# Row maxima of an attention kernel computed in one step per period, partly in spare columns of the scores' PSUM banks

## The chip, the cores and the metric

The kernel runs on one core of a Trainium2 chip. The metric is the device time of one execution in microseconds. The engines are called by the names of the profile: PE is TensorE's matmuls and PEld its weight loads, DVE is VectorE, ACT is ScalarE, POOL is GpSimd, SP is SyncE, which here only issues DMAs.

## What is computed

Two blocks follow each other. The first is attention with routing over 4 batches, 8 heads, 768 positions and head dimension 64. Each query and each key is assigned to the nearest of 16 centroids of its head, and a query sees only the keys of its own cluster. The second is a feed-forward layer on 3,072 tokens with the gate h * erf(softplus(h)).

```
mask   = q_assign[:, :, :, None] == k_assign[:, :, None, :]
scores = scale * q @ k.T
scores = where(mask, scores, -1e9)
attn   = exp(scores - max(scores)); attn /= sum(attn) + 1e-9
x      = (attn @ v) reshaped to (3072, 512)
h      = x @ w_in            # 512 -> 2048
out    = (h * erf(softplus(h))) @ w_out
```

This document is about the `max(scores)` of the first block: for every query a value to subtract ahead of the exponential.

## The kernel before, in words

**Pairs, units and periods.** Two heads are worked on together as a pair; there are 16 pairs (`NPAIR`). The two heads lie on partitions 0 to 63 and 64 to 127 of every operand, so that their matmuls use different rows of the array and run beside each other (`e` is 0 or 1 in the code). A pair's queries are cut into two halves of 384 (`HW`), its keys into six tiles of 128 (`NJ`). A unit `u` is one tile of keys against one half of the queries, so a pair has 12 units. A period (`period(p, i)`, line 1023) does two units, and a pair has six periods, i = 0 to 5. The order of instructions is the one in which the code is written: all engines are wrapped in `InOrder` (line 116), which keeps program order on each of them. Waits between engines are not written by hand: the tile framework puts them in, from the tiles that instructions read and write.

**A unit's way.** `products(u)` (line 500) multiplies a tile of keys with half the queries in fp32 and puts the result into a buffer `sc` of two PSUM banks, one for each head, 384 of 512 columns in each. `scores(u)` (line 513) adds a bf16 matmul of `km` and `qm` into the same columns: one row of them carries the shift (the maximum to be subtracted), the others the routing mask as very large numbers. `curve(u)` (line 527) is the exponential on ScalarE, from `sc` into a buffer `pr`. `attend(u)` (line 548) multiplies it with the values, one period later, into a bank `turned`; `accumulate(u)` (line 536) sums the exponentials on GpSimd, and `divide` (line 561) finishes a half: a matmul with `minus`, two curves on ScalarE, then three steps on VectorE.

**The maxima, three periods ahead.** `maxima_step(p, i)` (line 449) forms the bf16 scores again in the other orientation, 128 queries (a query tile t) on the partitions against 384 keys in the columns, in two passes, `qv` with `kv` (the scores themselves) and `qm` with `km` (the mask). Its output is `wide`, a tile of two PSUM banks, of which 384 columns each are used. VectorE reduces it to the maxima `nmx`. `step_ahead(u)` (line 1010) calls it for a step that lies 6 units ahead. Each period has two such steps: one for the first half of the keys, at its start, and one for the second half, whose passes are put around `scores` (`second`, lines 1050 to 1063). The second pass of the latter uses only rows 32 to 63 of each head's 64, so that it runs beside `scores`, which uses rows 0 to 31. When three query tiles are done, `lowest` takes the smallest over the pieces (the values are negated), and `turn` (line 480, called at i = 0 and 3) brings them into a row: six matmuls with an identity into `turned`, and two copies on ScalarE of one row each into row 0 of `qm`. The `scores` of the same period read that row.

**What lies around it in a period.** In the order of the code: `turn` and the first step ahead; a mask matmul (`mask(0)`); part of `divide`; the products of both units; `mask(1)`; the second step's first pass; scores; the rest of the second step; `mask(2)`; the two exponentials; preparation of weights for the second block on ScalarE, VectorE and GpSimd (`bounded`, `sign`, `shifted`, `size_and_rest`, `summed`, in most pairs); routing of a later pair (`choose`, `similarities`, `vectors`, `transposes`); then `accumulate`, `attend` and `divide` of the two units before. `choose` (line 393) writes its group maxima into columns 488 to 511 of a score buffer, which nothing else uses.

**PSUM.** Eight banks: two are `turned`, two are `wide` (line 175), and four are the two buffers of pool `ps_s` (line 174), which hands them out as tiles `sc` in turn (line 505).

Of the kernel before, what the change touches and what calls it, by code (L numbers as in the profile page):

```python
# [9 lines left out]
F32 = mybir.dt.float32  # L10
# [4 lines left out]
ALU = mybir.AluOpType  # L15
ACT = mybir.ActivationFunctionType
AX = mybir.AxisListType
PSUM = bass.MemoryType.PSUM

P = 128  # L20
B, H, S, D = 4, 8, 768, 64
C = 16
NJ = S // P
Q = 32
NB = S // Q
HW = S // 2
QW = HW // 2
TW = QW + 2
HJ = NJ // 2
HP = H // 2  # L30
NPAIR = B * HP
# [101 lines left out]
def kernel(  # L133
# [13 lines left out]
    te, ve, ae, ge = (  # L147
        InOrder(tc, e, in_order) for e in (nc.tensor, nc.vector, nc.scalar, nc.gpsimd)
    )
# [8 lines left out]
    turned = [ps.tile([P, 512], F32, name=f"turned{i}") for i in range(2)]  # L158
# [12 lines left out]
    def passing(name, bufs, **kw):  # L171
        return attention.enter_context(tc.tile_pool(name=name, bufs=bufs, **kw))

    ps_s = passing("ps_s", 2, space=PSUM)
    wide = passing("ps_w", 1, space=PSUM).tile([P, 2, 512], F32, name="wide")

    const = passing("fixed", 1)
# [12 lines left out]
    lowest = [const.tile([P, HJ, P], BF16, name=f"lowest{i}") for i in range(2)]  # L190
# [255 lines left out]

    turns = []

    def maxima_step(p, i, sm=wide, behind=False):

        st = pairs[p]
        nmx = maxima[p % 2]
        t, half = divmod(i, 2)

        def passes(a, b, start, rows):
            for e in range(2):
                r = slice(e * D + rows.start, e * D + rows.stop)
                te.matmul(
                    sm[:, e, 0:HW], lhsT=st[a][r, t * P : (t + 1) * P],
                    rhs=st[b][r, half * HW : (half + 1) * HW], start=start, stop=not start,  # L460
                )

        passes("qv", "kv", True, slice(0, D))
        if behind:
            yield
        passes("qm", "km", False, slice(Q, D) if behind else slice(0, D))
        if behind:
            yield
        ve.tensor_reduce(
            out=nmx[:, :, t, half], in_=sm[:, :, 0:HW], axis=AX.X, op=ALU.max, negate=True  # L470
        )
        if i in (NJ - 1, 2 * NJ - 1):
            h = i // NJ
            ve.tensor_reduce(
                out=lowest[h][:, :, ::D].rearrange("p t e -> p e t"),
                in_=nmx[:, :, h * HJ : (h + 1) * HJ], axis=AX.X, op=ALU.min,
            )
            turns.append((p, h))

    def turn(p, h, copies=(ae.copy, ae.copy)):  # L480

        st = pairs[p]
        pn = turned[h][:, 0:HW].rearrange("p (t n) -> p t n", t=HJ)
        for t in range(HJ):
            for e in range(2):
                cols = slice(e * D, e * D + Q)
                te.matmul(pn[cols, t], lhsT=lowest[h][:, t, cols], rhs=identb, start=True, stop=True)
        for e, copy in zip(range(2), copies):
            r = slice(e * D, e * D + 1)
            copy(out=st["qm"][r, h * HW : (h + 1) * HW], in_=pn[r].rearrange("p t n -> p (t n)"))  # L490
        st["shift", h] = True
# [8 lines left out]
    def products(u):  # L500
        p, half, j = units[u]
        if u in sc_of:
            return
        st = pairs[p]
        sc = sc_of[u] = ps_s.tile([P, 2, 512], F32, name="sc", tag="s")
        for e in range(2):
            r = slice(e * D, (e + 1) * D)
            te.matmul(
                sc[:, e, 0:HW], lhsT=st["kT"][r, j * P : (j + 1) * P],
                rhs=st["qT"][r, half * HW : (half + 1) * HW], start=True, stop=False,  # L510
            )

    def scores(u, rows=Q):

        p, half, j = units[u]
        st = pairs[p]
        sc = sc_of[u]
        assert ("shift", half) in st
        for e in range(2):
            r = slice(e * D, (e + 1) * D)  # L520
            r = slice(r.start, r.start + rows)
            te.matmul(
                sc[:, e, 0:HW], lhsT=st["km"][r, j * P : (j + 1) * P],
                rhs=st["qm"][r, half * HW : (half + 1) * HW], start=False, stop=True,
            )
# [478 lines left out]
    def run(work):  # L1004
        for _ in work:
            pass

    def step_ahead(u, behind=False):  # L1010
        p, i = divmod(u + NJ, 2 * NJ)
        steps = maxima_step(p, i, behind=behind) if p < NPAIR else iter(())
        if not behind:
            run(steps)
        return steps

    forms = []
    for f in range(0, HF, 2):
        forms += zip(*(left_forms(e, *w_in_parts(f, 2)) for e in (ve, ge)))
# [3 lines left out]
    def period(p, i):  # L1023
        u = 2 * NJ * p + 2 * i
        n1, n2 = 2 * p - 1, 2 * p
        early = lambda n: 0 <= n < N_EARLY

        def mask(place):
            which = (MASKS if p else FIRST_MASKS).get((i, place))
            if which:  # L1030
                return masks(p + 1, *which, turned[0 if i in (0, 5) else 1], place > 1, ve if i == 0 else ae)
            return lambda: None

        if u > 0:
            for which in turns if i in (0, 3) else ():
                turn(*which)
                turns.remove(which)
            step_ahead(u)
        mask(0)()
        next(part[0], None)  # L1040
        if i == 5:
            next(routing[0], None)
        if i == 0 and p:
            run(routing[0])
        if u == 2:
            next(routing[0])
        products(u)
        products(u + 1)
        mask(1)()
        second = step_ahead(u + 1, True) if u > 0 else iter(())  # L1050
        next(second, None)
        rows = D if u == 0 or u + NJ >= len(units) else Q
        scores(u, rows)
        next(second, None)
        if i:
            next(second, None)
        next(part[0], None)
        scores(u + 1, rows)
        later = mask(2)
        if i == 0:  # L1060
            later()
            later = lambda: None
            next(second, None)
        if i == 3:
            similarities(p + 2)
            routing[0] = choose(p + 2, sc_of[u + 1][:, 0], True)
        curve(u)
        later()
        curve(u + 1)
        if u == 0:  # L1070
            step_ahead(1)
            similarities(1)
            routing[0] = choose(1, turned[0])
            next(routing[0])
            next(routing[0])
            vectors(1, "q")
            vectors(1, "k")
        if i == 0 and early(n1 - 1):
            bounded(n1 - 1)
            shifted(n1 - 1)  # L1080
            sign(n1 - 1)
        elif i == 1 and early(n1):
            size_and_rest(n1)
        elif i == 3 and early(n1):
            bounded(n1)
            sign(n1)
        elif i == 5 and early(n2):
            rest(n2)
        for _ in range(min(len(forms), FORMS.get(p, {}).get(i, 0))):
            forms.pop(0)[0]()  # L1090
        if i == 3:
            next(routing[0], None)
            if early(n1):
                shifted(n1)
            for _ in range(2):
                next(routing[0], None)
        elif i == 1:
            load(p + 1, "v", v, vp)
            if p == 0:
                run(routing[0])  # L1100
                transposes(2, "q")
        elif i == 2:
            transposes(p + 2, "k")
        elif i == 4:
            vectors(p + 2, "k")
            vectors(p + 2, "q")
        elif i == 5:
            transposes(p + 3, "q")
        if u > 0:
            if i == 1 and early(n1 - 1):  # L1110
                summed(n1 - 1)
            elif i == 4 and early(n1):
                summed(n1)
            for w in (u - 2, u - 1):
                accumulate(w)
            if i % HJ == 1 and p in POOL_FORMS and forms:
                forms.pop(0)[1]()
            for w in (u - 2, u - 1):
                attend(w)
            if i % HJ == 0:  # L1120
                part[0] = divide(u - 1)
                next(part[0])
        if i == 3 and early(n2):
            size(n2)
# [25 lines left out]
    for r in (0, D):  # L1150
        for half in range(2):
            for e in range(2):
# [2 lines left out]
                    out=pick[r : r + D, half, e * D : (e + 1) * D].rearrange("p (n c) -> p n c", n=2)[:, :, 1 : C + 1],  # L1155
                    in_=first[r : r + D, c : c + C].unsqueeze(1).to_broadcast([D, 2, C]),
                )
    also = ps_s.tile([P, 2, 512], F32, name="sc", tag="s")
    products(0)
    warm(9, turned[0], zeros)  # L1160
    run(choose(0))
# [9 lines left out]
    for n in range(PLACES - 1):  # L1171
        fetch(n)
    for i in range(NJ):
        run(maxima_step(0, i, also if i % 2 else wide))
        if i == 1:
            masks(0, "q", 1, turned[1])()
        if i < NJ - 1:
            warm(2, turned[0], zeros)
    step_ahead(0)
    warm(2, turned[0], zeros)  # L1180
    turn(0, 0, (ae.copy, ve.tensor_copy))
    turns.clear()
# [124 lines left out]
```

## Time and profile before

| | |
|---|---|
| median of 3 runs | 978.78 us (978.75 to 978.95) |
| the profiled execution | 978.7 us |
| its span on the core | 976.8 us |
| attention stage | up to about 408.5 us of the span |
| feed-forward stage | from about 408.5 us on |
| one pair of heads, for example 90.54 to 115.00 us | 24.46 us |
| TensorE busy in the span | 968.1 us |
| VectorE busy in the span | 757.9 us |
| ScalarE busy in the span | 526.8 us |
| one reduction of `wide` (768 elements per partition) | 955 ns on average |
| one exponential (768 elements per partition) | 812 ns on average |

How to read it: almost every instruction has the line of the helper that records it (124), so groups are told apart by the names of tiles, written as output <- inputs. In a group's line stand its count, then its busy time and the mean length of one, then the idle time of its engine just ahead of it and what ended that idle time. A timeline line has its start, its length, its engine, what it does, how many instructions are merged in it, and in brackets the idle time before them. In the table of waits stand the total, the number of times and the longest. Where a stretch of the span is given, its columns are the length of the stretch, then each engine's busy time (PE, PEld, DVE, ACT, POOL), the granted clock of TensorE, the share of the DMA engines and GB/s.

### The profile page before, as it was taken

The numbers are of one execution on the slowest core, as the hardware profiler recorded it, in microseconds if no ns is written. First come the engines' busy times: TensorE is split into PE (matmuls) and PEld (weight loads), VectorE is DVE, ScalarE is ACT, GpSimd is POOL, SyncE is SP. The second block draws the span as 40 slices with busy tenths as digits, with TensorE's granted clock in tenths as the row PEclk, the third lists the DMA queues.
The fourth block names the chain that finished last, engine by engine and source line by source line (L and its number), as shares of the span: only waits on it lengthen the run. The fifth ranks groups of instructions, "written<-read, shape, count | busy, mean of one in ns | idle before, by whom it ended". The sixth has DMA issues, their size and how long they took to land.

```text
span 976.8 us, 20838 instructions
## 1 busy us (share of the span) xinstructions
PE 968.1 (99%) x8282; PEld 724.4 (74%) x8282; DVE 757.9 (78%) x1431; ACT 526.8 (54%) x799; POOL 409.9 (42%) x277
## 2 busy tenths in 40 slices
PE   8999999999999999999999999999999999999998
PEld 3555555555555555688888888888888888888887
DVE  8888888888888886879788786568666856685766
ACT  3777777777777665377623430562165235413541
POOL 1688887788888888853199600000000000000000
PEclk9999999999999999999999999999999999999999
DMA  9444444444444211142004544023302420241023
GB/s 216 81 110 110 109 109 109 107 110 109 87 110 110 54 35 34 47 152 87 0 22 173 200 140 134 1 65 129 108 0 87 129 87 1 65 145 50 1 86 108
DMA packets 157185, 88.42 MB, mean 91 GB/s; under 512 B 129696, under 2 KB 139424, under 8 KB 157088
## 3 DMA queue, kind: packets, MB, share of 16 engines
q1 hardware_dynamic: 154736, 86.80, 32.2%
q8 instruction: 65, 1.06, 0.5%
q10 hardware_dynamic: 2352, 0.30, 0.2%
q14 instruction: 32, 0.26, 0.1%
HBM read 68.19 MB, written 18.87 MB: 89 GB/s over the span
## 4 chain that ended last, share of the span: by engine, by line
PE 97%; DVE 1%; SPq 1%; issue 0%; DMA 0%; ACT 0%; DVEq 0%
PE bank L124 43%; PE turned L124 31%; PE sc L124 17%; PE wide L124 6%; SPq L124 1%; DVE nmx L124 1%; DMA in_q<-in_q_dram 0%; DVE kT L124 0%; DVE qT L124 0%; DVE km L124 0%; DVE turned L124 0%; DVE sims L124 0%; ACT qm L124 0%; DVE g_more L124 0%; DVE osb L124 0%
## 5 line engine op out<-in xcount | busy, mean ns | idle before, releaser
L124 POOL TENSOR_TENSOR more_out<-more_out,pr 128x768 f32<-128x768 f32 x128 | 217.0, 1696 | 18.7 <-ACT pr L124 10.1
L124 DVE TENSOR_REDUCE nmx<-wide 128x2 f32<-128x768 f32 x189 | 180.5, 955 | 48.2 <-PE wide L124 47.2
L124 ACT ACTIVATE pr<-sc 128x768 f32<-128x768 f32 x192 | 148.9, 812 | 94.2 <-PE wide L124 78.6
L124 PE MATMUL turned<-pr,in_v 128*32 128x194 f32 x3072 | 145.5, 330 | 0.0
L124 DVE TENSOR_TENSOR g<-bank,g 128x256 f32<-128x256 f32 x222 | 89.5, 419 | 54.5 <-PE bank L124 34.6
L124 PEld LDWEIGHTS turned<-pr,in_v 128*32 128x32 f32 x3072 | 91.5, 109 | 51.2 <-issue 21.3
L124 DVE TENSOR_TENSOR g<-g 128x512 f32<-128x512 f32 x114 | 78.8, 692 | 42.3 <-PE bank L124 32.2
L124 PE MATMUL bank<-x_own,w_in 128*128 128x256 f32 x424 | 104.4, 379 | 0.0
L124 PE MATMUL sc<-qT,kT 64*128 64x384 f32 x528 | 98.3, 486 | 0.0
L124 PEld LDWEIGHTS bank<-x_own,w_in 128*128 128x128 f32 x424 | 80.4, 190 | 11.5 <-issue 0.6
L124 ACT ACT_TABLE_LOAD x48 | 61.6, 1283 | 38.2 <-DVE g L124 37.5
L124 DVE TENSOR_TENSOR g<-a_s,g 128x512 f32<-128x512 f32 x96 | 74.1, 786 | 3.8 <-ACT a_s L124 3.8
L124 PE MATMUL bank<-x_more,more_in 128*128 128x256 f32 x296 | 76.0, 379 | 0.0
L124 PE MATMUL bank<-w_out,g 128*128 128x256 f32 x328 | 75.7, 379 | 0.0
L124 POOL TENSOR_TENSOR more_out<-pr,pr 128x768 f32<-128x768 f32 x32 | 60.2, 1880 | 28.3 <-ACT pr L124 28.3
L124 PE MATMUL bank<-g_more,g 128*128 128x256 f32 x296 | 69.9, 379 | 0.0
L124 PEld LDWEIGHTS bank<-w_out,g 128*128 128x128 f32 x328 | 62.3, 190 | 8.5
L124 PEld LDWEIGHTS <-qv 64*128 64x128 bf16 x384 | 27.0, 93 | 52.8 <-issue 36.7
L124 PEld LDWEIGHTS sc<-qT,kT 64*128 64x128 f32 x528 | 50.0, 187 | 21.2 <-ACT inv L124 2.3
L124 PE MATMUL wide<-kv,qv 64*128 64x384 bf16 x378 | 64.1, 328 | 1.3 <-DVE nmx L124 0.6
L124 PE MATMUL wide<-km,qm 64*128 64x384 bf16 (+1 forms) x378 | 62.6, 327 | 0.0
L124 PEld LDWEIGHTS bank<-g_more,g 128*128 128x128 f32 x296 | 56.2, 190 | 7.6
(195 smaller groups left out, 1746.1 us busy)
## 6 DMA issues: line engine op xcount, KB each, us to landing
g_more<-b_dram SPq DMA_DIRECT2D x48, 512.0 KB, 3.3
x_own<-in_moe_w_in_dram SPq DMA_DIRECT2D x13, 512.0 KB, 4.5
in_v<-in_v_dram SPq DMA_DIRECT2D x32, 192.0 KB, 3.1
x_dram<-more_out SPq DMA_DIRECT2D x128, 48.0 KB, 2.0
x_own<-x_dram SPq DMA_DIRECT2D x6, 1024.0 KB, 5.3
in_k<-in_k_dram SPq DMA_DIRECT2D x59, 96.0 KB, 2.8
in_q<-in_q_dram SPq DMA_DIRECT2D x58, 96.0 KB, 2.8
out_dram<-osb SPq DMA_DIRECT2D x20, 256.0 KB, 3.3
```

Of the source, the lines that this page charges most:

```text
L124: ins = getattr(self.engine, name)(*args, **kw)
```

## The change

Five things change, all within the attention stage.

- The four banks of the scores become one tile `sc4`, taken once: two units by two heads by 512 columns. The buffer of unit u is `sc4[:, u % 2]`. The 128 columns from 384 on (`HW:`) in each of the four banks were spare.
- A period now finds the maxima of one query tile over all 768 keys in one step, `bounds(p, t)`: keys 0 to 511 in the two banks of `wide`, keys 512 to 639 in the spare columns of the even unit's banks, and 640 to 767 in those of the odd unit's banks. Two reductions follow, one of 1,024 elements per partition over `wide`, one of 512 over all four spare pieces. Before there were two of 768.
- The passes of the step are put in one bf16 group behind the products: first pass for `wide` and both spare pieces, then the second passes and the scores. All second passes use 32 rows: `wide` rows 32 to 63, the spare pieces rows 0 to 31, as the scores do. [...]
- `turn` and `mask(0)` move from before the products to behind them. Products are now the first matmuls of a period.
- `choose` for pair p + 2 puts its group maxima into the same columns of `turned[0]` rather than of a score buffer.

The last pair's later periods, which have no maxima to find, and the start of the kernel keep the old steps. The core of the diff:

```diff
-    ps_s = passing("ps_s", 2, space=PSUM)
+    sc4 = passing("ps_s", 1, space=PSUM).tile([P, 2, 2, 512], F32, name="sc")
...
+    def bounds(p, t):
+
+        st, nmx = pairs[p], maxima[p % 2]
+        outs = {"wide": wide, 0: sc4[:, 0, :, HW:], 1: sc4[:, 1, :, HW:]}
+        keys = {"wide": slice(0, 512), 0: slice(512, 512 + P), 1: slice(512 + P, S)}
+
+        def passes(at, a, b, rows, start, stop):
+            for e in range(2):
+                r = slice(e * D + rows.start, e * D + rows.stop)
+                te.matmul(
+                    outs[at][:, e], lhsT=st[a][r, t * P : (t + 1) * P], rhs=st[b][r, keys[at]],
+                    start=start, stop=stop,
+                )
+
+        def first_of(at):
+            passes(at, "qv", "kv", slice(0, D), at == "wide", False)
+
+        def second_of(at):
+            beside = at == "wide"
+            passes(at, "qm", "km", slice(Q, D) if beside else slice(0, Q), False, beside)
+
+        def reduced():
+            ve.tensor_reduce(out=nmx[:, :, t, 0], in_=wide, axis=AX.X, op=ALU.max, negate=True)
+            ve.tensor_reduce(
+                out=nmx[:, :, t, 1:3].rearrange("p e c -> p c e"), in_=sc4[:, :, :, HW:],
+                axis=AX.X, op=ALU.max, negate=True,
+            )
+            if t % HJ == HJ - 1:
+                lowest_of(p, t // HJ)
+
+        return first_of, second_of, reduced
...
-        sc = sc_of[u] = ps_s.tile([P, 2, 512], F32, name="sc", tag="s")
+        sc = sc_of[u] = sc4[:, u % 2]
...
-        if u > 0:
-            for which in turns if i in (0, 3) else ():
-                turn(*which)
-                turns.remove(which)
-            step_ahead(u)
-        mask(0)()
         next(part[0], None)
...
         products(u)
         products(u + 1)
-        mask(1)()
-        second = step_ahead(u + 1, True) if u > 0 else iter(())
-        next(second, None)
-        rows = D if u == 0 or u + NJ >= len(units) else Q
-        scores(u, rows)
-        next(second, None)
-        if i:
-            next(second, None)
-        next(part[0], None)
-        scores(u + 1, rows)
+        for which in turns if i in (0, 3) else ():
+            turn(*which)
+            turns.remove(which)
+        mask(0)()
+        ahead, tile_of = divmod(i + HJ, NJ)
+        ahead += p
+        if u == 0 or ahead >= NPAIR:
+            mask(1)()
+            scores(u, D)
+            scores(u + 1, D)
+            reduced = lambda: None
+        else:
+            first_of, second_of, reduced = bounds(ahead, tile_of)
+            for at in ("wide", 0, 1):
+                first_of(at)
+            mask(1)()
+            if i in (0, 3):
+                for at in (0, "wide", 1):
+                    second_of(at)
+                scores(u)
+                scores(u + 1)
+            else:
+                second_of("wide")
+                second_of(0)
+                scores(u)
+                second_of(1)
+                scores(u + 1)
         later = mask(2)
         if i == 0:
             later()
             later = lambda: None
-            next(second, None)
+        reduced()
+        next(part[0], None)
         if i == 3:
             similarities(p + 2)
-            routing[0] = choose(p + 2, sc_of[u + 1][:, 0], True)
+            routing[0] = choose(p + 2, turned[0], True)
         curve(u)
         later()
         curve(u + 1)
```

## The prediction

> **What bounds the kernel now.** I read the page first, then the waits and the busy times of the attention stage, then the timeline of single periods. The page's busy times and its chain of work, with two of its groups:
>
> ```profile
> PE 968.1 (99%) x8282; PEld 724.4 (74%) x8282; DVE 757.9 (78%) x1431; ACT 526.8 (54%) x799; POOL 409.9 (42%) x277
> ...
> PE 97%; DVE 1%; SPq 1%; issue 0%; DMA 0%; ACT 0%; DVEq 0%
> ...
> L124 DVE TENSOR_REDUCE nmx<-wide 128x2 f32<-128x768 f32 x189 | 180.5, 955 | 48.2 <-PE wide L124 47.2
> L124 ACT ACTIVATE pr<-sc 128x768 f32<-128x768 f32 x192 | 148.9, 812 | 94.2 <-PE wide L124 78.6
> ```
>
> TensorE is the bound: the maxima's reductions and the exponentials wait for it, not it for them. The waits between 42.91 and 384.88 us (pairs 1 to 14) say the same, and so does the table of busy times for pairs 1 to 11 (269.26 of 269.50 us busy):
>
> ```profile
> ACT pr L124 <- PE wide L124: 69.7, 70, 2.2
> ...
> PE wide L124 <- DVE nmx L124: 0.2, 1, 0.2
> ```
>
> ```profile
> 42.90:312.40 269.50, 269.26 (x3881) 153.30 (x3874) 230.90 (x375) 210.31 (x341) 215.66 (x133) 1.00 0.48 107
> ```
>
> A pair takes 269.5/11 = 24.50 us, six periods. The timeline of one (i = 3):
>
> ```profile
> 105.69 0.33 PE L124 MATMUL wide<-kv,qv 64*128 64x384 bf16 x2
> 105.95 0.33 PE L124 MATMUL sc<-qm,km 32*128 32x384 bf16 x2
> 105.95 0.34 PE L124 MATMUL wide<-km,qm 32*128 32x384 bf16 x2
> 106.12 0.32 PE L124 MATMUL sc<-qm,km 32*128 32x384 bf16 x2
> ...
> 106.39 0.96 DVE L124 TENSOR_REDUCE nmx<-wide 128x2 f32<-128x768 f32 x1 [0.83 <-PE wide L124]
> 106.41 1.51 ACT L124 ACTIVATE pr<-sc 128x768 f32<-128x768 f32 x2 [1.15 <-PE wide L124]
> ...
> 107.81 1.38 ACT L124 ACTIVATE x_own<-x_own 128x512 int16<-128x512 f32 x1
> ...
> 108.40 0.55 DVE L124 TENSOR_REDUCE sc<-sims 128x24 f32<-128x384 f32 x1
> ...
> 108.99 0.56 DVE L124 TENSOR_TENSOR hot<-sims,sc 128x384 bf16<-128x384 f32 x1
> ```
>
> The reduction (VectorE) and the two exponentials (ScalarE) start together at 106.4, side by side, and end by 107.9, while TensorE runs the values' matmuls. A pair of 384-column bf16 matmuls takes 0.16 us; going from 64-row to 32-row tiles adds 0.10 (105.69 to 105.95). One place has a reader of the scores' spare columns already, `hot`. The weight loads at 109.66 are of a product into that bank, other columns:
>
> ```profile
> 109.66 0.31 PEld L124 LDWEIGHTS sc<-qT,kT 64*128 64x128 f32 x3 [0.34 <-ACT inv L124]
> ```
>
> They start 0.11 us after `hot` ends (109.55), though the two touch different columns. In the last pair no maxima stand between the values' matmuls and the next products:
>
> ```profile
> 400.11 0.53 PE L124 MATMUL turned<-more_out,minus 128*32 128x192 f32 x8
> 400.57 1.56 PE L124 MATMUL sc<-qT,kT 64*128 64x384 f32 x8
> 401.97 0.49 PE L124 MATMUL sc<-qm,km 64*128 64x384 bf16 x4
> ```
>
> There the products take 1.40 us to the next matmul, against 1.29 in mid-stage (104.40 to 105.69): their fp32 weights are not loaded ahead over the change of tile shape.
>
> [...]
>
> **The change, part by part.** Times are from the first product of a period (0).
>
> *Passes.* Before, 160 each for qv, qm, qv, with the second qm beside the scores, and 320 for the scores: 800 ns. After, 768 columns of qv are 320; then wide's qm (213) runs beside 53 + 160 of the scores' row group, then 53 + 160 more: 746. It saves 54 ns. Products directly after values cost 0.10 (above; at best nothing). [...]
>
> *The turn* (i = 0 and 3) moves behind the products. Between values and maxima it added 0.16; between two 64-row groups it adds 0.28 and one more change, 0.09. Its two ScalarE casts (0.94) were hidden by the products; now only the first passes lie between, so the scores wait until 1.39 + 0.09 + 0.34 (turn with its drain) + 0.09 + 0.94 + 0.10 = about 2.95; the passes alone (turn 0.37, first passes 0.33, tile change 0.10, two small pairs 0.13 after the products' 1.39) would let them start at 2.33.
>
> *Waits.* This decides. The built changed kernel lists, for each instruction, the semaphores it waits for. In 93 of 96 periods the first exponential waits for VectorE; in the kernel before none does. Its count is the one that the spare columns' reduction raises, which is behind the wide reduction in VectorE's queue. And the first product of the next period waits for that reduction and for the *second* exponential, where before it waited for the first alone (95 periods). So reductions, exponentials and products, side by side until now, stand in a row; behind the waiting product on TensorE's queue is everything else of the period. Behind the waiting exponential is ScalarE's whole queue.
>
> *One period* (i = 1, 2, 4, 5 bare): products 1.39; first passes 0.33; tile change 0.10; wide's qm record, 0.34 for 384 columns, with 53 ns for 128 more and its start 0.40; to VectorE 0.08 (median of the 82 reductions that waited). The reduction starts at 2.30. Between 384 elements (550 ns) and 768 (955) the slope is 1.055 ns, so 1,024 take 1.22 and 512 take 0.69 [...]; with 0.02 between, 1.93. To ScalarE 0.10, two exponentials 1.51, to TensorE 0.12. Sum 5.96 us. Values end near 3.7, so TensorE then idles 2.2. The bare period before was 3.78 (96.19 to 99.97).
>
> The six: **i = 0**: scores at 2.96, mask done at 3.46, its VectorE copy (620 ns) is ahead of both reductions: 4.18 + 3.66 (reductions, exponentials, hand-overs) = 7.84. **i = 3**: wide's qm starts 0.38 later, 6.34. **i = 2**: mask matmul of 0.16 before the passes and a mask copy between the exponentials (they then take 1.98): 6.59. **i = 5**: mask copy 0.48, 6.35. **i = 1 and 4** while weights are prepared (pairs 1 to 11): ScalarE does the sign (1.38) after the exponentials, then the divide's two curves, then VectorE three steps, all ahead of the next wide reduction: 3.0 us from the exponentials' end in the trace, so it starts at 2.90 and the period is 6.56; else 5.96.
>
> *Sum.* Pairs 1 to 11: 7.84 + 6.56 + 6.59 + 6.34 + 6.56 + 6.35 = 40.24 each, 442.6 for 269.5: +173.1. Pairs 12 to 14: 39.04 each, 117.1 for 72.5: +44.6. Pair 0, five periods: 31.4 for 20.7: +10.6. Pair 15, three periods 18.3 for 11.8 (+6.5), and its last three, with casts and the second exponential waited for, +1.6. In all +236. The feed-forward stage has 4.5 us of idle TensorE at most to give and no changed line: 0. The profiled run is 978.7 us (span 976.8 and 1.9 around it), the median 978.78, so **1215 us**. VectorE's, GpSimd's and ScalarE's other steps, the chooser's move to `turned` and the DMAs lie in TensorE's idle time; if that cover were gone, they would cost at most what they cost in 40 us a pair, of which VectorE is busy 21.
>
> **Rivals.** *The waits lie beside TensorE's work.* Then only the passes, the weight load and the turn count: per pair 4 x 0.05 + 2 x 0.85 = 1.9, about 1008 us. For it: VectorE and ScalarE waited before. Against: 3.6 us of row does not fit in 1.45 of values. *Products wait for the first exponential alone*: 0.70 less in 92 periods, 1148. The listed count speaks against. *The clock falls*: [...] *Faster*: the 54 ns are kept and reductions and exponentials still run side by side, ending within the 1.45 us of values; products then wait for nothing, the fp32 load hides, and 92 x 0.054 = 5 gives 974. It decides if the listed count is raised before the scores end; the count belongs to an instruction that starts after them. That the maxima are not computed in one step can be excluded from the listing.
>
> **How the numbers follow.** The forecast 0.80 (1170 to 1245 by its own bounds: hand-overs 4 x 0.05 x 92 = 18 either way, products' load hidden -9, sign delay absent -13, [...]); first exponential alone 0.07; clock 0.08; beside TensorE 0.03; faster 0.02. Range 1170 to 1250. A measurement of this kernel can tell about 0.2% from no change; faster 0.02, within it 0.01, slower 0.97.
>
> **What would show it.** Right: ACT pr waiting for DVE nmx some 90 times; products waiting for ACT pr, 2 us each; TensorE near 65% busy in the stage; a 1,024-element reduction near 1.22 and one of 512 near 0.69; the pair near 40 us, the turn's period longest. Wrong: exponentials that start before the spare reduction ends, a clock below 1.00, or a pair below 27 us.

## The result, and the profile after

The change makes the kernel slower: **1245.13 us** (median of 4 runs, 1245.02 to 1254.62) against 978.76 us for the kernel before, a ratio of 1.275 (95% interval 1.272 to 1.277). The profiled execution took 1245.02 us, with a span of 1243.3 us. The forecast was 1215 with a range of 1170 to 1250: the sign and most of the size were right, and 30 us are missing from the sum.

All of it lies in the attention stage. From the first matmul of the feed-forward stage to the end it is 568.4 us in both traces; of the last 568.30 us TensorE is busy 563.73 after and 563.78 before. The parts of the page that answer to those shown of before: busy times, granted clock, the chain, and the two groups of maxima and exponentials.

```profile
PE 1037.5 (83%) x8650; PEld 742.5 (60%) x8650; DVE 753.9 (61%) x1431; ACT 534.1 (43%) x799; POOL 407.5 (33%) x277
...
PEclk9998899898989999998989999999999999999999
...
PE 68%; DVE 13%; ACT 12%; issue 6%; DMA 0%; ACTq 0%; DVEq 0%; SPq 0%
...
L124 ACT ACTIVATE pr<-sc 128x768 f32<-128x768 f32 x192 | 148.8, 811 | 257.9 <-DVE nmx L124 253.1
L124 DVE TENSOR_REDUCE nmx<-wide 128x2 f32<-128x1024 f32 (+1 forms) x97 | 117.4, 1210 | 180.4 <-PE wide L124 179.1
```

No engine is full any more: TensorE is down from 99% to 83%, and VectorE and ScalarE have a quarter of the chain that ended last, where they had 1%. An exponential is as long as before (811 ns against 812). What grew is the idle time ahead of it: 257.9 us instead of 94.2, and its releaser is no longer TensorE but the reduction `nmx`. Yet TensorE's busy time *rose* by 69 us, for 368 more but mostly small matmuls. That is the first hint that part of them ran slowly, and the clock row shows it: dips to 8 tenths, all in the first 22 of 40 slices, the attention stage.

The waits of the whole span, each with its total, its number of times and its longest, in us:

```profile
ACT pr L124 <- DVE nmx L124: 253.1, 92, 4.6
...
PEld sc L124 <- ACT pr L124: 188.2, 81, 2.8
...
PE sc L124 <- ACT pr L124: 157.4, 80, 2.4
...
PEld turned L124 <- DVE hot L124: 44.0, 14, 3.4
...
PE turned L124 <- DVE hot L124: 34.3, 14, 2.7
```

The first three are the row that was predicted: exponentials wait for the reduction 92 times, and the products wait for exponentials 80 times, 157.4/80 = 2.0 us each. The last two were not predicted. Fourteen times, once in each pair that still has a routing ahead, the values' matmuls wait 2.5 us on average for `hot`, the last step of `choose`.

The end of a period with that wait and the whole one after it, in the timeline (start, length, engine, what it does, and in brackets the idle time before it; "..." stands for lines left out):

```profile
422.23 0.85 PE L124 MATMUL turned<-more_out,ccT 128*32 128x384 f32 x8
...
425.02 0.55 DVE L124 TENSOR_TENSOR hot<-sims,turned 128x384 bf16<-128x384 f32 x1
...
425.63 1.52 PE L124 MATMUL turned<-pr,in_v 128*32 128x194 f32 x32 [2.56 <-DVE hot L124]
...
427.41 1.56 PE L124 MATMUL sc<-qT,kT 64*128 64x384 f32 x8
...
428.80 0.38 PE L124 MATMUL wide<-kv,qv 64*128 64x512 bf16 x2
...
429.23 0.39 PE L124 MATMUL wide<-km,qm 32*128 32x512 bf16 x2
...
429.52 0.32 PE L124 MATMUL sc<-qm,km 32*128 32x384 bf16 x2
429.66 1.23 DVE L124 TENSOR_REDUCE nmx<-wide 128x2 f32<-128x1024 f32 x1
...
429.77 1.52 PE L124 MATMUL turned<-pr,in_v 128*32 128x194 f32 x32
430.80 0.68 DVE L124 TENSOR_REDUCE nmx<-sc 128x4 f32<-128x512 f32 x1
...
431.58 1.51 ACT L124 ACTIVATE pr<-sc 128x768 f32<-128x768 f32 x2 [2.63 <-DVE nmx L124]
...
433.14 1.56 PE L124 MATMUL sc<-qT,kT 64*128 64x384 f32 x8 [1.85 <-ACT pr L124]
```

Read the lower half first, the bare period (one without a turn or extra work in the row) from 427.41 to 433.14. Each link starts where the one before it ends: reductions 429.66 to 431.48, exponentials 431.58 to 433.09, products at 433.14. Before, reduction and exponentials both started at 106.4. TensorE ends its values at 431.29 and then has nothing for 1.85 us. Now the upper lines: VectorE still reads `turned` for `hot` until 425.57, and the values, which write other columns of that bank, start 0.06 us after it, having waited 2.56 us.

Periods of pairs 1 to 11 by their place in the pair, from first product to first product, in us. "Shortest" is the shortest of the eleven and stands for the undisturbed length; in these two kernels the clock was at full speed in it.

| | i = 0 | 1 | 2 | 3 | 4 | 5 | sum |
|---|---|---|---|---|---|---|---|
| before, shortest | 4.09 | 3.78 | 4.08 | 4.73 | 3.81 | 3.93 | 24.43 |
| forecast | 7.84 | 6.56 | 6.59 | 6.34 | 6.56 | 6.35 | 40.24 |
| after, shortest | 7.54 | 6.31 | 6.36 | 8.48 | 5.73 | 6.11 | 40.54 |
| after, mean | 7.59 | 6.70 | 6.36 | 9.45 | 5.94 | 6.21 | 42.26 |

Mean and shortest are 0.07 apart in a pair before, and 1.72 after. Two neighbouring stretches of about one pair each, and one later, show why (length, then busy time of PE, PEld, DVE, ACT, POOL, then the granted clock):

```profile
57.85:99.71 41.86, 27.76 (x378) 14.89 (x376) 20.79 (x34) 19.77 (x31) 19.61 (x13) 0.96 0.28 64
99.71:146.02 46.31, 33.37 (x380) 16.77 (x378) 20.90 (x34) 19.75 (x31) 19.53 (x13) 0.82 0.25 58
399.80:440.75 40.95, 28.00 (x378) 14.75 (x377) 20.90 (x34) 19.80 (x31) 19.56 (x13) 0.96 0.25 52
```

The same work, with VectorE, ScalarE and GpSimd equally busy to 0.15 us, takes TensorE 33.37 us at a mean clock of 0.82 and some 28 at 0.96. These means are made of two clocks. Two neighbouring pieces of the third stretch, in the same columns:

```profile
403.41:406.82 3.41, 1.01 (x10) 0.69 (x8) 1.51 (x4) 2.54 (x4) 0.00 (x0) 1.00 0.51 115
406.82:410.23 3.41, 3.41 (x32) 1.45 (x32) 2.28 (x5) 0.73 (x3) 3.05 (x2) 0.50 0.27 76
```

TensorE has little to do in the first piece, at the full clock, and runs the second at half the clock. The same place, i = 4 of a pair, in the timeline:

```profile
402.93 0.51 PE L124 MATMUL turned<-more_out,minus 128*32 128x192 f32 x8
...
405.84 2.02 PE L124 MATMUL sc<-qT,kT 64*128 64x384 f32 x8 [2.40 <-ACT pr L124]
...
409.40 1.90 PE L124 MATMUL turned<-pr,in_v 128*32 128x194 f32 x32
```

After 2.40 us of idleness come products that take 2.02 us instead of 1.56, since the clock falls within them at 406.82, and then values that take 1.90 instead of 1.52, since it comes back within them at 410.23.

By this trace's record of the clock, the half clock comes in pieces of 3.41 us, all on one grid of 3.41 us. The attention stage has 26 of them after its first 20 us, 19 in pairs 1 to 11; the stretch at 0.82 has five, the other two stretches one each. In 22 of the 24 places where the clock fell, TensorE had been busy for at most 1.51 us of the grid's piece just before. Of the 142 pieces at full clock that no fall followed, all but one held 1.50 us of work or more. So what counts here is how little TensorE does in such a piece. Whether a period's gap makes a piece that empty depends on how the gap lies on the grid, and so pairs with the same work differ.

### The profile page after: what moved, and what is told of

Read it like the earlier page. It is cut to its first block, busy times and chain, and to the rows that moved or that the text cites. A ratio compares the mean times of both kernels' runs of the same rounds, so it can differ in the third digit from the quotient of the medians.

```text
span 1243.3 us, 21607 instructions
## 1 busy us (share of the span) xinstructions
PE 1037.5 (83%) x8650; PEld 742.5 (60%) x8650; DVE 753.9 (61%) x1431; ACT 534.1 (43%) x799; POOL 407.5 (33%) x277
## 4 chain that ended last, share of the span: by engine, by line
PE 68%; DVE 13%; ACT 12%; issue 6%; DMA 0%; ACTq 0%; DVEq 0%; SPq 0%
PE bank L124 34%; PE turned L124 16%; PE sc L124 14%; ACT pr L124 10%; DVE nmx L124 9%; PE wide L124 4%; ACT qm L124 2%; DVE km L124 1%; DVE turned L124 1%; DVE hot L124 1%; DVE sims L124 1%; ACT km L124 1%; DVE w_in L124 0%; ACT x_own L124 0%; DMA in_q<-in_q_dram 0%
## 5 line engine op out<-in xcount | busy, mean ns | idle before, releaser
L124 ACT ACTIVATE pr<-sc 128x768 f32<-128x768 f32 x192 | 148.8, 811 | 257.9 <-DVE nmx L124 253.1
L124 DVE TENSOR_REDUCE nmx<-wide 128x2 f32<-128x1024 f32 (+1 forms) x97 | 117.4, 1210 | 180.4 <-PE wide L124 179.1
L124 PE MATMUL sc<-qT,kT 64*128 64x384 f32 x528 | 110.0, 536 | 106.3 <-ACT pr L124 106.3
L124 PE MATMUL turned<-pr,in_v 128*32 128x194 f32 x3072 | 158.5, 351 | 34.3 <-DVE hot L124 34.3
L124 PEld LDWEIGHTS turned<-pr,in_v 128*32 128x32 f32 x3072 | 94.7, 116 | 92.3 <-DVE hot L124 44.0
L124 PEld LDWEIGHTS sc<-qT,kT 64*128 64x128 f32 x528 | 47.1, 193 | 150.1 <-ACT pr L124 127.3
L124 PE MATMUL sc<-more_out 64*128 64x384 f32 x240 | 54.5, 579 | 51.1 <-ACT pr L124 51.1
L124 PE MATMUL sc<-qm,km 32*128 32x384 bf16 (+1 forms) x384 | 64.7, 347 | 5.8 <-ACT qm L124 5.5
L124 DVE SCALAR_TENSOR_TENSOR den<-turned,inv 128x192 f32<-128x192 f32 x31 | 11.1, 358 | 92.4 <-ACT inv L124 92.4
L124 PEld LDWEIGHTS sc<-more_out 64*128 64x128 f32 x240 | 22.9, 206 | 71.8 <-ACT pr L124 60.9
```

Source lines behind the costliest of these rows:

```text
L124: ins = getattr(self.engine, name)(*args, **kw)
```

## Experiments

**Theory.** Sharing banks puts reductions, exponentials and products in a row; the 30 us that the forecast lacks are `choose` in `turned[0]` and stretches at a lower clock. **Rivals.** The single step itself costs this much, wherever its output lies; or the time is one of amount, of more matmuls and longer reductions; or `choose` is covered by other idleness, as the prediction said.

The first five go at the row and at the two surprises.

### Maxima kept out of the scores' banks

This kernel leaves out the maxima over keys 512 to 767. VectorE's second reduction reads 512 elements of `wide` again, so its work is unchanged.

```diff
-                out=nmx[:, :, t, 1:3].rearrange("p e c -> p c e"), in_=sc4[:, :, :, HW:],
-                axis=AX.X, op=ALU.max, negate=True,
+                out=nmx[:, :, t, 1], in_=wide[:, :, 0:256], axis=AX.X, op=ALU.max, negate=True
...
-            for at in ("wide", 0, 1):
+            for at in ("wide",):
```

> Leaves out part of the computation: the maxima over keys 512 to 767 of every query tile done in one step, and their matmuls. In their place VectorE reduces 512 elements of wide once more, so that its work stays what it is in the changed kernel, but no longer touches the scores' banks. Theory (a reduction in the scores' banks holds up the exponentials, and these the products): exponentials start beside the reductions again; products still wait for the second exponential, since the scores are still one tile, and in i = 3 the values still wait for the chooser. Bare period 3.8 us, i = 0 5.1, i = 3 9.0, pair about 30 us, about 1090 us in all. Rival (it is the amount and place of the reductions, not the bank): only the four small pairs of matmuls are saved, 0.24 us a period, about 1223 us.

Measured: **1083.8 us** (one run). The bare period fell from 5.73 to 3.88, and the exponentials wait for TensorE's scores again; its waits:

```profile
ACT pr L124 <- PE sc L124: 55.6, 69, 2.4
...
PEld sc L124 <- ACT pr L124: 51.2, 81, 0.9
...
PEld turned L124 <- DVE hot L124: 42.4, 14, 3.1
```

So 161 us of the 266 come from where a third of the maxima lies. VectorE reduces as many elements as in the changed kernel, so its amount is not the reason. The missing bf16 matmuls cannot be it either: in the changed kernel such pairs of 128 columns start some 56 ns apart, and four pairs make 0.2 us of the 1.85. Products still wait for exponentials 81 times, since the scores are still one tile, but for 0.6 us each instead of 2.3. The wait for `hot` stays, at full size, and i = 3 is not shorter but longer (shortest 9.66 for 8.48): in all of pairs 1 to 11 a piece at half clock falls into it.

### The chooser's maxima out of PSUM

Only the place of `choose`'s group maxima differs from the changed kernel: a tile in SBUF.

```diff
-        mx = (wide[:, 0] if spare is None else spare)[:, 512 - n :]
+        mx = routep.tile([P, n], F32, name="mx")
```

> The chooser's group maxima go to a small SBUF tile instead of columns 488 to 511 of turned[0]. Theory (in i = 3 the values' matmuls into turned[0] wait for the chooser's reduction and comparison because they share its bank, which the prediction had taken as hidden): i = 3 falls from 8.5 to about 6.2 us, i = 4 grows from 5.7 to about 6.6 because the divide's curves are then late, about 1.4 us less in each of 14 pairs, about 1225 us. Rival (the wait lies in idle time of TensorE, as the prediction said): 1245 us, no change.

Measured: **1224.11 us** (1222.81 to 1224.72; ratio to before 1.251, 1.248 to 1.253), 21.0 less than the changed kernel, as the theory said. The shortest i = 3 went from 8.48 to 6.12. In exchange i = 4 went from 5.73 to 6.30: in the changed kernel the longer i = 3 had given the weights' preparation time to finish, which i = 4 otherwise waits for. Net 1.8 us per pair, 14 pairs, 25 us. The clock stayed at 0.964.

### TensorE kept busy after the first values

Zero weights into `turned`, twice a unit's values' matmuls, in each period of the changed kernel; they add nothing to the result.

```diff
-            for w in (u - 2, u - 1):
-                attend(w)
+            attend(u - 2)
+            idle_work(u - 2)
+            attend(u - 1)
```

> Adds work that changes no result: after the first of the two value groups of a period, the same matmuls twice more with weights of zero, 1.3 us of TensorE's idle 2.2 us. Theory (the granted clock falls in windows of idleness, and this costs some 18 us): clock 1.00 throughout, all full pairs near 40.8 us, about 1227 us. Rival (the slow clock falls where TensorE would have waited anyway): clock 1.00 and 1245 us. Third (the added matmuls are themselves in the way in i = 1 and 3): 1250 us or more.

Measured: **1256.52 us** (1253.79 to 1258.05), ratio 1.284 (1.282 to 1.285). The time did not fall. The trace shows two effects. The periods other than i = 3 are all at their undisturbed length (means within 0.1 of the shortest), as they would be if idleness lowered the clock. But the added matmuls stand behind the wait for `hot`, where they cannot fill the gap, and come after it: i = 3 went from 9.45 to 10.96 on average, and from 8.48 to 9.79 at its shortest. All pieces at half clock in pairs 1 to 11 lie in i = 3. This kernel mixes both causes and settles neither.

### Both together

The same added matmuls, with the chooser's maxima in SBUF.

> The chooser's maxima in SBUF, as in the run chooser_sbuf, and the matmuls with weights of zero after the first value group, which change no result. The clock's part alone: in the earlier filled run every period but i = 3 stood at its undisturbed length, and i = 3 only because of the chooser's wait. Theory (slow windows cost time and go when the idle stretches are shorter): clock 1.00, a pair at 38.7 us, the sum of the undisturbed periods, about 1194 us. Rival (the added matmuls cost as much as the clock gave): 1224 us or more.

Measured: **1203.98 us** (1203.6 to 1204.01), ratio 1.230 (1.228 to 1.232). The granted clock of the kernel without and with the added matmuls:

```profile
core 0: 1222.3 us, clock 0.964
```

```profile
core 0: 1202.3 us, clock 0.999
```

Added work made the kernel 20.1 us shorter. The mean pair is now within 0.04 us of the shortest (39.12 and 39.08), while without the added matmuls the two are 2.15 apart (40.88 and 38.73): 2.15 x 11 = 24 us in pairs 1 to 11. No piece at half clock is left in the attention stage. Only work was added, so the lower clock came from TensorE having too little to do. I had expected 1194: the added matmuls are in the way at i = 3, which grew by 0.91, while i = 4 fell by 0.57.

### The second reduction done twice

On the changed kernel, the reduction of the spare columns is issued two times in a row, with the same output.

```diff
+            ve.tensor_reduce(
+                out=nmx[:, :, t, 1:3].rearrange("p e c -> p c e"), in_=sc4[:, :, :, HW:],
+                axis=AX.X, op=ALU.max, negate=True,
+            )
```

> The reduction of the spare columns is done twice in every period. Theory (the reduction stands in one row with the exponentials and products): 0.70 us more in each of 92 periods, about 1310 us. Rival (it runs beside them): 1245 us.

Measured: **1367.34 us** (one run). The bare period grew from 5.73 to 6.48, by 0.75, about one more reduction (0.68), so the reduction is on the path in full. The clock fell further:

```profile
core 0: 1365.6 us, clock 0.914
```

The periods i = 0, 1, 2 and 4 grew by 0.73 to 0.75 at their shortest. In i = 3 and 5 every one of pairs 1 to 11 has some half clock, so their shortest does not stand for an undisturbed length here. At 0.75 in 92 periods the row itself makes 69 of the 122 us more; the 53 that remain go with the lower clock, which was not added up pair by pair. My expectation had only the first.

### The spare columns reduced first

If the exponentials wait for the spare reduction because it is second in VectorE's queue, then putting it first takes 1.2 us out of the row. On the kernel with the chooser in SBUF:

```diff
-            ve.tensor_reduce(out=nmx[:, :, t, 0], in_=wide, axis=AX.X, op=ALU.max, negate=True)
             ve.tensor_reduce(
                 out=nmx[:, :, t, 1:3].rearrange("p e c -> p c e"), in_=sc4[:, :, :, HW:],
                 axis=AX.X, op=ALU.max, negate=True,
             )
+            ve.tensor_reduce(out=nmx[:, :, t, 0], in_=wide, axis=AX.X, op=ALU.max, negate=True)
```

> chooser_sbuf with the two reductions of a period in the other order: the spare columns first, wide second. Nothing else changes, and the exponentials still wait for the spare reduction alone. Theory (all that stands ahead of the exponentials on VectorE counts): the spare reduction starts when the scores end, at 2.5 us of a period, the exponentials at 3.3 instead of 4.2; a bare period 4.9 instead of 5.7, about 1.0 us less on average, 1125 to 1140 us. Rival (the wait for the wide reduction is what decides, through the next period's passes into wide): no change, 1224 us.

Measured: **1122.23 us** (one run), 102 less than the 1224.11 of its base, with a clock of 0.999. A swap of two lines, with no instruction more or less. The exponentials' wait is shorter (254.5 us in 92 waits in the base):

```profile
ACT pr L124 <- DVE nmx L124: 139.5, 79, 3.4
...
PEld sc L124 <- ACT pr L124: 127.8, 81, 1.8
```

i = 1 fell from 6.30 to 5.17. With the row 1.1 us shorter, the idle stretch is too, and the clock stays up without added work: 102 us are (38.73 - 33.95) x 15 = 72, plus some 23 of clock in pairs 1 to 11 and a rest in the other pairs.

### One tile of scores for each unit

The four banks become two tiles of two banks, and the spare reduction is cut into two of 256 elements, ahead of the wide one.

```diff
-    sc4 = passing("ps_s", 1, space=PSUM).tile([P, 2, 2, 512], F32, name="sc")
+    ps_s = passing("ps_s", 1, space=PSUM)
+    scs = [ps_s.tile([P, 2, 512], F32, name=f"sc{i}") for i in range(2)]
...
+            for c in range(2):
+                ve.tensor_reduce(
+                    out=nmx[:, :, t, 1 + c], in_=scs[c][:, :, HW:], axis=AX.X, op=ALU.max, negate=True
+                )
             ve.tensor_reduce(out=nmx[:, :, t, 0], in_=wide, axis=AX.X, op=ALU.max, negate=True)
...
-        sc = sc_of[u] = sc4[:, u % 2]
+        sc = sc_of[u] = scs[u % 2]
```

> chooser_sbuf, with the scores in two tiles, one for each unit of a period, and the spare reduction in two halves, one for each tile, both ahead of the wide one. Now the first exponential waits for 256 elements, the second for the other 256, and the first product of the next period for the first exponential alone. Same work otherwise. Theory: a bare period 3.9 to 4.0 us, i = 0 5.6, i = 1 5.1, i = 3 5.9 (casts of the turn and the mask's copy on VectorE), pair about 29 us, about 1050 us, clock 1.00. Rival (any reader of the score banks costs the whole row): 1120 us or more.

Measured: **1051.52 us** (one run), 71 less again. The end of a period in its trace:

```profile
202.62 0.75 DVE L124 TENSOR_REDUCE nmx<-sc 128x2 f32<-128x256 f32 x2
203.13 1.52 ACT L124 ACTIVATE pr<-sc 128x768 f32<-128x768 f32 x2 [1.61 <-DVE nmx L124]
...
204.00 1.62 PE L124 MATMUL sc<-qT,kT 64*128 64x384 f32 x8 [0.51 <-ACT pr L124]
```

The first exponential starts before both small reductions have ended (203.37), and the products start before both exponentials have (204.65). In the changed kernel they started 0.05 us after the second one, though they write the banks of the first. The period is 4.07 at i = 4 (6.30 in the base, 3.81 in the kernel before) and 4.91 at i = 1. Only i = 3 missed the expectation by much: 6.99 for 5.9. The two tiles and the halved reductions came in one edit, so the 71 us are not divided between them.

### And the turn ahead of the products again

```diff
-        products(u)
-        products(u + 1)
         for which in turns if i in (0, 3) else ():
             turn(*which)
             turns.remove(which)
+        products(u)
+        products(u + 1)
```

> split_banks with the turn ahead of the products again, as in the kernel before. Theory (the turn's casts are hidden by the products again, the four other periods are unchanged): i = 0 about 4.9, i = 3 about 5.1, pair about 27.5 us, about 1025 us; still slower than 979, since products directly after values cost 0.10 each period and the reductions of 256 stand ahead of the exponentials. Rival (casts were hidden anyway): as split_banks.

Measured: **1040.62 us** (1040.29 to 1040.75), ratio 1.063 (1.061 to 1.065). Less than expected was won: i = 0 and 3 fell by 1.3 each, but i = 2 and 5 grew by some 0.95 each. A part of that is only the turn itself, which now lies ahead of the first product and so counts to the period before. The rest is a wait, as the timeline at such a place shows:

```profile
204.46 0.19 DVE L124 TENSOR_REDUCE lowest<-nmx 128x6 bf16<-128x18 f32 x1
204.70 0.34 PE L124 MATMUL turned<-identb,lowest 128*32 128x128 bf16 x6 [0.61 <-DVE lowest L124]
```

The wide reduction now stands last, `lowest` waits for it, and a turn at the start of the next period waits for `lowest`, with the products queued behind it. It is the fastest kernel here that uses the spare columns, and still 6% slower than the kernel before. The exponentials still wait for reductions, 141.9 us in 92 waits.

The last two put one part of the change alone into the kernel *before*.

### The chooser's move alone

```diff
-            routing[0] = choose(p + 2, sc_of[u + 1][:, 0], True)
+            routing[0] = choose(p + 2, turned[0], True)
```

> The kernel before with one part of the change alone: the chooser's group maxima of pair p + 2 in columns 488 to 511 of turned[0]. Theory (the values of i = 3 go into turned[0] and wait until the chooser has read its maxima): in 14 pairs the values of i = 3 start at the end of the chooser's comparison, 109.6 instead of 107.0 us in the pair looked at, 2.6 us more each, about 1014 us. Rival (the chooser's place costs nothing as long as nobody else is in a row with it): 979 us.

Measured: **1018.36 us** (1018.19 to 1019.43), ratio 1.041 (1.039 to 1.042). i = 3 grew from 4.73 to 7.31, 2.58 in 14 pairs: 36 of 39.6 us; the lower clock, 0.992, makes most of the rest, 0.33 a pair in pairs 1 to 11. Its waits show the same line as the changed kernel:

```profile
PEld turned L124 <- DVE hot L124: 42.0, 15, 3.1
...
PE turned L124 <- DVE hot L124: 32.0, 14, 2.4
```

### The turn behind the products alone

```diff
-            for which in turns if i in (0, 3) else ():
-                turn(*which)
-                turns.remove(which)
...
+        for which in list(turns) if u > 0 and i in (0, 3) else ():
+            turn(*which)
+            turns.remove(which)
```

The loop goes from ahead of the first step to just behind both products; the steps stay.

> The kernel before with another part alone: the turn behind the products instead of before the first step ahead, which stays where it is. Theory (a group of another tile shape between two 64-row groups, 0.2 us, and the scores waiting for the two casts on ScalarE, of which only 0.54 us of matmuls hide a part, 0.9 us): 1.1 us in each of 31 turns, about 1013 us. Rival (the casts were off the path): 0.2 us each, 985 us.

Measured: **1011.35 us** (1011.0 to 1011.53), ratio 1.033 (1.031 to 1.035). i = 0 grew from 4.09 to 5.33 and i = 3 from 4.73 to 5.95, while i = 2 and 5 fell by 0.15 each, as the turn no longer lies at their end. The whole pair grew from 24.43 to 26.53: 2.10 in 15 pairs are 31.5 of the 32.6 us.

## Why the prediction was right where it was, and where it was not

**The row of waits: right.** It rested on two listed waits, the first exponential on the spare reduction and the first product on the second exponential. The trace has 92 of the first, and the products wait 2.0 us each. TensorE is 28.00/40.95 = 68% busy in the third stretch, for a forecast near 65. Taking the spare columns away took the bare period from 5.73 to 3.88; doubling the second reduction lengthened it by 0.75; putting that reduction first shortened i = 1 by 1.13. Three edits, and each moved the period by about the instruction's own length or what the row predicts.

**The links: right, a little too long.** Reductions of 1.23 and 0.68 (forecast 1.22 and 0.69), exponentials 1.51 (1.51), products 1.39 from 427.41 to 428.80 (1.39); their weight loads start with them, at 427.41, where in mid-stage before, for the products at 104.40, they start 0.16 us ahead, at 104.24. The bare period is 5.73 and not 5.96. The reductions start 2.25 after the first product (2.30), and the second starts 1.14 after the first, before that one's record ends, where I had set 1.24. The exponentials start 0.10 after the reductions; from their start to the next product it is 1.56 where I had 1.63. I had added whole records and whole hand-overs, which overlap a little. 0.23 in 92 periods is 21 us too many. It hid part of what was missing. A smaller slip changed nothing: 0.70 less in 92 periods makes 1151, not 1148.

**The chooser's move: wrong, a term put at nothing.** The prediction put it with the steps that "lie in TensorE's idle time". That treats it as VectorE's work, with room to be done in. But what it moves is a wait: from the scores' bank to `turned[0]`, which the values need in the same period. In the old place weight loads of the products idled 0.34 us, by the prediction's reading because of `hot`; in the new one the values, and TensorE's whole queue with them, stand behind `hot`: 2.58 us in the kernel before, a net 1.8 per pair in the changed one, 21.0 us by the run without it. The prediction had the evidence in hand. It showed that products wait for `hot` through other columns of one bank, and did not ask who waits next once `hot` reads another bank.

**The clock: a rival that came true in part.** The prediction forecast 2.2 us of idleness for each bare period and gave the lower clock 0.08, as a case of its own. In fact it comes on top of the row in some pairs: 1.72 a pair, 19 us in pairs 1 to 11, about 1 us for each of the 19 pieces at half clock there. That it falls with idleness was an estimate of mine; the trace of before, with a clock of 1.00, did not show it. Nor was TensorE idle for a whole piece: it was busy 1.01 us of the 3.41 us before the fall at 406.82. Little work was enough: at most 1.51 us of such a piece ahead of 22 of the 24 falls. With the gaps filled, the clock was 0.999.

**The sum.** 1215, less 21 for links taken too long, plus 25 for the chooser, plus 19 for the clock, gives 1238. (The run without the chooser's move gained 21 and not 25, since it loses more to the clock, 2.15 a pair for 1.72.) The 7 that remain fit the seven pieces at half clock in pairs 0 and 12 to 15, at the same 1 us each; this is an estimate. So 51 us were left out and 21 put in too many. That the measured time lies within the range, 5 us from its upper end, is in part luck: with the links right, the forecast would have been 1194.

**The turn: right in kind.** The forecast made i = 0 the longest, because scores wait for the two casts that the products hid. In the trace the casts end at 401.13, and three of the four matmuls of the scores start from 401.19 on. The period is 7.54 (7.84), the longest in the run with the chooser's maxima in SBUF. Alone in the kernel before the turn costs 2.10 a pair, 1.05 for each of the two.

**The other rivals.** "Beside TensorE's work" (1008) falls with the row. "Products wait for the first exponential alone" (1148) falls too: the products at 433.14 start 0.05 us after the second exponential ends. "Faster" (974) rested on reductions and exponentials side by side; no period shows it.

Open: the row comes from waits that the framework puts in, and the runs do not tell whether they follow the bank or the tile. In every kernel here the columns that were shared lay in one tile of the program; that the tile counts is shown by the two tiles for the two units, since with one tile the products waited for an exponential of other banks. A version in which two engines use one bank at once was not tried, and no run here shows what would happen.

## What to carry to other kernels

Spare columns of a PSUM tile that is in use were not free here (161 of the 266 us): in these kernels everyone who read or wrote any column of such a tile joined one row, and a tile over several banks made each of them wait for all. Before a step is moved, list the banks (not the columns) that it touches in the new place and who needs them in the same period; ask this of the small helper step too, since it cost 40 us alone. When a tile must be shared, put the sharing piece first in its engine's queue and give each unit's banks a tile of their own: here these two edits took back 173 of the 245 us left without the chooser's move, without changing what is computed.

## What was unexpected in the hardware

- TensorE's clock did not sink gradually. It was halved for pieces of 3.41 us on a fixed grid, and this happened though TensorE was never idle for a whole piece: in the changed kernel mostly after a piece with at most 1.51 us of work, and in the kernel before with the chooser's move alone after pieces with 1.37 to 1.69 us, while no other piece of that stage after its first 20 us had less than 1.70. With the spare columns reduced first, no 3.41 us of the stage after its first 25 us held less than 1.84 us of work, and the clock stayed at 0.999. A few falls in the changed kernel do not fit (two after 1.96 and 2.11 us), so the exact measure stays open.
- So added matmuls with zero weights made a kernel 20.1 us faster (1224.11 to 1203.98).
- Lengthening a row by 0.7 us a period cost 122 us where the row alone makes some 69: longer idleness also lowered the mean clock, from 0.964 to 0.914.
